# All queues of a fused attention and expert kernel in another written order, with 16 filling products at the start

## The chip, the cores and the metric

The kernel runs on one core of a Trainium2 chip. The metric is device time in microseconds (us) of one execution. Every operation is issued by one of the core's engines: TensorE (PE in the profile, its weight loads PEld), VectorE (DVE), ScalarE (ACT), GpSimd (POOL) and SyncE (SP, which only issues DMAs here; ScalarE and GpSimd issue some too).

## What is computed

```python
# q, k, v: 8 batches, 8 heads, 576 positions, 64 dimensions
scores = q @ k.T / 8                       # per head
local   = (rel >= 0) & (rel < 32)          # heads 0..3, rel = query - key
strided = (rel >= 0) & (key % 32 == query % 32)   # heads 4..7
x = softmax(where(mask, scores, -1e9)) @ v        # x: 8 x 576 x 512, heads side by side
logits = x @ w_gate                        # 4 experts, the best 2 of each token
for e in range(4):                         # a causal attention head of 64 dimensions each
    y = softmax(causal(x @ wq[e] @ (x @ wk[e]).T / 8)) @ (x @ wv[e]) @ wo[e]
    out += weight[e] * y                   # softmax over the two best logits, 0 for others
```

## The kernel before

The work of a batch falls into two stages. Stage 1 handles heads in pairs (`hp` 0 to 3; 0 and 1 local, 2 and 3 strided). Queries and keys are loaded, turned so that the head dimension lies on partitions (`load_big`, `tp`, `tp_out` for batch 0 and part of batch 1; VectorE's `turn` or `turn_s`, L574, for the others), and multiplied block by block (`s_l`, `s_s`). In batches 0 and 1 the mask is added by a product in the same bank ahead of the scores (`pre`, L646). The row softmax has six steps: `softmax0` maximum (VectorE), `softmax1` subtraction, `softmax2` exponential (ScalarE, L697), `softmax3` sum, `softmax4` reciprocal (both VectorE), `softmax5` scaling (L708, on VectorE or GpSimd in batches 0 and 1, on GpSimd later). The probabilities are turned by VectorE (`turn`, L722) or TensorE (`pt`, `pt_out`), multiplied by the values (`xa_l`, `xa_s`) and split into a rounded part `xh` and a rest `xl`.

Stage 2 multiplies these by the expert weights, which are split in the same way (`hi_w`, `lo_w`, L453 and L456): `pj` for queries and keys (three products for each K tile), `vp` for values and gate. `gate1` (GpSimd), `gmax`, `gate2`, `gate3` (VectorE, L907 to L909) and `gate5` (GpSimd) make the experts' weights. `s2` are the scores, `max2`, `exp2`, `recip2` and `scale2` their softmax, `t2` the transposes, `acc` the product with the values, `oh` and `ol` its split, `yp` the product with `wo` and `store` the output.

Nothing is scheduled by a planner at run time. Each operation gets a number when it is declared (`op`), and the text `PLAN` lists all of them in one order. A word such as `85P1511` is operation 85 on TensorE (P; A is ScalarE, D VectorE, G GpSimd, S SyncE) and the buffer numbers that it takes, one digit for each new buffer. `schedule` walks the list, so each engine's queue has its operations in the order of the words with its letter, and waits come from the dependencies. Engines work in order: a waiting operation holds all behind it. Copies out of PSUM may stand on ScalarE or VectorE, loads on SyncE, GpSimd or (the first) ScalarE.

`warm` (2) is a row of products on constants that stands first on TensorE; it reads `fz`, which `one` (0) sets on VectorE. It writes the eight banks, then six of them again, 328 columns each. `fill` operations (2625 and up; `NF` of them) are single products of 448 columns whose result nobody reads. They stand in the list wherever its writer put them.

```python
    def spin(i):
        wb = RB.new(f"spin{i}")
        op("fill", "P", 448, 0, lambda e: ones(wb, 448), r=[fz], w=[wb], mode=M128)
```

Of the kernel before, what the change touches and what calls it, by code (L numbers as in the profile page):

```python
# [20 lines left out]
def attention_moe_kernel(  # L21
# [72 lines left out]
    NF = 26  # L94
# [26 lines left out]
    def issuer(e):  # L121
# [13 lines left out]
        2643P1 2644P1 2645P1 2646P1 2647P1 2648P1 2649P1 85P1511 160A 183S2 121D 159A 52D 122G 148S 228P240 54D  # L135
        86A 88A 230D 179G0 123P760 89D 180S 225P34 87D 192G 125A 1209P50 226A 124D 227A 1202P1 162D 195S3 150G
        229D 126P6322 191D0 149S 184A 1246P71 127A 131D 292G1 129A 161D 1260P4 186S 181A 236P2 208G1 163D 237P0
        182D 363S2 193A 130D 128D 90G 132D 165G 151S 1210P 239D0 164G 241D 1247P 293S 238D 1203P 185G 194D
        1266P6 146S 290G 166P321 187A 212S 1261P 167A 168D 328G3 196A 198S 1211P 240D 287G 1248P 188D 288S 197D
        1267P 205S 286G 169P3233 291S 209G 213A0 1204P 330S 172A 174A 173D 170A 1253P0 331G 329S 175D 242A 1254P  # L140
        171D 202G 1255P 243D 1222P2 365S 1256P 327G4 244D 325S 1262P 199A 1212P 300S2 200G 1216P3 1214A0 1205P
        214G0 1257A 294D1 231S1 206A 1268P 324G 1223P 210A 1206A 1269P 295D 369S0 1258A1 207G 1249P 1207A 326S
        1224P 1270A 337G0 1271A 302P0 1213D 255S1 303P1 1250D 304P0 203A 1251D 253S 211D 340P5 472G1 1217P 306D1
        204D 1225P 368S 20G012345 305D 1263P 232S 1272D0 1252G 1233P70 307D 1264A 473S 1227A 333D0 1226A 367G
        1259G 1235P6 308D 434S3 332D 176G 309A 245G 366S 1218P 1236A 341P0 1265D 1234A 397S4 342P1 435G 310D
        299S 1273P1601 55G 344D2 133G 233G 1361P740 334S 1228D1 19D0 346D 254G 297S 343D 1229P2 1363D0 1215G
# [1102 lines left out]
```

## Time and profile before

| | us |
|---|---|
| median of 3 runs | 432.48 (432.35 to 433.54) |
| the profiled execution | 432.82 |
| its span, first to last instruction | 431.1 |
| TensorE busy | 421.2 |
| VectorE busy | 344.3 |
| GpSimd busy | 322.6 |
| ScalarE busy | 241.5 |

Times in the rows count from the start of the span. Matmuls are pipelined, and their ends are modelled: a row's duration is longer than the time that the next product waits for it, and a started matmul can make TensorE look busy while the following one waits. Durations of VectorE and ScalarE operations overlap their neighbours' by some 0.08 us. A row of the timeline with "x14" is a run of 14 instructions, and its second figure is the time from the first one's start to the last one's end. In square brackets stands the idle time before a row and what ended it. "PEclk" is the granted TensorE clock as a share of full speed.

### The profile page before, as it was taken

How to read it: one execution, taken by the hardware profiler on the slowest of the kernel's cores; microseconds unless marked ns; L12 is line 12 of the kernel's file. 1: busy time of each engine (PE TensorE's matmuls, PEld its weight loads, DVE VectorE, ACT ScalarE, POOL GpSimd, SP SyncE). 2: the span in 40 equal slices, each digit the busy share in tenths (PEclk: the TensorE clock that was granted, in tenths of full speed). 3: DMA queues.
4: the chain of work that ended last, by engine and by line, in shares of the span. 5: the costliest groups of instructions: out<-in, count | busy, mean ns of one | idle time of the engine just before them, and what ended most of it. 6: DMA issues, size and time to landing. Idle time of an engine off the chain costs nothing.

```text
span 431.1 us, 18683 instructions
## 1 busy us (share of the span) xinstructions
PE 421.2 (98%) x7506; PEld 369.0 (86%) x7506; DVE 344.3 (80%) x1046; ACT 241.5 (56%) x753; POOL 322.6 (75%) x554
## 2 busy tenths in 40 slices
PE   8899998999999999999999999999999999999996
PEld 5679877999788988899888997999898998997875
DVE  2897999899998799999898989766998768453734
ACT  3555277654964567545774355626791367466840
POOL 7899876999996978898799925996888232935900
PEclk9999999999999999999999999999999999999999
DMA  8986755564745625774433615245221100003014
GB/s 178 214 171 127 144 120 98 114 128 91 132 88 96 142 55 127 158 145 80 85 79 65 148 33 123 63 117 120 65 58 61 50 26 2 2 26 100 27 75 147
DMA packets 145951, 41.78 MB, mean 97 GB/s; under 512 B 137600, under 2 KB 139008, under 8 KB 145864
## 3 DMA queue, kind: packets, MB, share of 16 engines
q1 hardware_dynamic: 139416, 32.05, 35.6%
q0 software_dynamic: 5856, 8.39, 7.9%
q8 instruction: 59, 0.97, 1.0%
q14 instruction: 28, 0.23, 0.2%
q10 hardware_dynamic: 592, 0.15, 0.1%
HBM read 31.11 MB, written 9.44 MB: 94 GB/s over the span
## 4 chain that ended last, share of the span: by engine, by line
PE 87%; DVE 5%; POOL 3%; issue 1%; DMA 1%; ACT 1%; SPq 1%; POOLq 0%; DVEq 0%; ACTq 0%
PE bank L936 21%; PE bank L1171 12%; PE bank L857 10%; PE bank L1136 10%; PE bank L1038 8%; PE bank L1103 7%; PE bank L780 3%; PE bank L803 2%; PE bank L635 2%; PE bank L628 2%; PE bank L990 2%; PE bank L865 2%; PE bank L732 2%; PE bank L947 1%; PE bank L760 1%
## 5 line engine op out<-in xcount | busy, mean ns | idle before, releaser
L1084 POOL TENSOR_SCALAR p<-p,st,wt 128x128 f32<-128x128 f32 (+3 forms) x128 | 76.5, 606 | 6.6 <-DVE st L1064 5.4
L1056 ACT ACTIVATE p<-p,st 128x128 f32<-128x128 f32 (+3 forms) x128 | 72.1, 567 | 14.0 <-DVE st L1051 14.0
L1051 DVE CUSTOM_DVE_ANT_0 p<-bank,m_cau 128x384 f32<-128x384 f32 (+3 forms) x128 | 57.1, 480 | 4.5 <-PE bank L1038 2.8
L574 DVE STREAM_TRANSPOSE qkt<-nat 128x576 f32<-128x576 f32 x52 | 52.9, 1026 | 1.4 <-issue 1.4
L324 ACT COPY th<-bank 128x256 f32<-128x256 f32 (+2 forms) x121 | 46.2, 444 | 11.9 <-PE bank L1103 8.7
L1136 PE MATMUL bank<-th,vs 128*64 128x192 f32 (+4 forms) x512 | 48.0, 337 | 0.1
L1136 PEld LDWEIGHTS bank<-th,vs 128*64 128x64 f32 x512 | 34.2, 137 | 14.3 <-issue 8.0
L857 PE MATMUL bank<-wh_v,xh 128*128 128x260 f32 x128 | 36.7, 286 | 0.0
L857 PE MATMUL bank<-wh_v,xl 128*128 128x260 f32 x128 | 36.3, 283 | 0.0
L857 PE MATMUL bank<-wl_v,xh 128*128 128x260 f32 x128 | 36.2, 283 | 0.0
L746 DVE TENSOR_TENSOR xl<-bank,xh 128x270 fp32r<-128x270 f32 (+4 forms) x104 | 32.4, 337 | 3.2 <-ACT xh L324 2.8
L1103 PE MATMUL bank<-ident,p 64*128 64x64 f32 x800 | 34.0, 228 | 0.7 <-POOL p L1084 0.6
L936 PE MATMUL bank<-xh,wh_k 128*128 128x288 f32 x112 | 34.2, 305 | 0.0
L1103 PEld LDWEIGHTS bank<-ident,p 64*128 64x128 f32 x800 | 29.4, 138 | 5.3 <-ACT th L324 0.9
L936 PE MATMUL bank<-xh,wh_q 128*128 128x288 f32 x112 | 33.5, 299 | 0.0
L936 PE MATMUL bank<-xl,wh_k 128*128 128x288 f32 x112 | 33.0, 295 | 0.0
L936 PE MATMUL bank<-xl,wh_q 128*128 128x288 f32 x112 | 33.0, 295 | 0.0
L936 PE MATMUL bank<-xh,wl_k 128*128 128x288 f32 x112 | 33.0, 295 | 0.0
L936 PE MATMUL bank<-xh,wl_q 128*128 128x288 f32 x112 | 33.0, 295 | 0.0
L324 ACT CAST qk<-bank 128x288 fp32r<-128x288 f32 x37 | 14.8, 404 | 29.7 <-PE bank L936 27.0
L965 POOL TENSOR_TENSOR qkl<-kf,qk 128x288 fp32r<-128x288 f32 x32 | 25.7, 809 | 2.2 <-DVE kf L324 1.9
L1171 PE MATMUL bank<-wh_o,oh 128*128 128x512 f32 (+1 forms) x66 | 26.5, 401 | 0.0
(191 smaller groups left out, 1330.8 us busy)
## 6 DMA issues: line engine op xcount, KB each, us to landing
out_dram<-ys SPq DMA_DIRECT2D x31, 256.0 KB
nat<-in_k_dram SPq DMA_DIRECT2D x74, 72.0 KB
nat<-in_q_dram SPq DMA_DIRECT2D x72, 72.0 KB
v<-in_v_dram SPq DMA_DIRECT2D x60, 40.0 KB
nat<-in_q_dram POOLq DMA_DIRECT2D x32, 72.0 KB, 3.0
v<-in_v_dram SPq DMA_DIRECT2D x96, 22.5 KB
nat<-in_k_dram POOLq DMA_DIRECT2D x30, 72.0 KB, 3.2
v<-in_v_dram SPq DMA_DIRECT2D x56, 27.0 KB
```

Source lines behind the costliest of these rows:

```text
L324: (nc.scalar.copy if e == "ACT" else nc.vector.tensor_copy)(dst, src)
L574: nc.vector.transpose(dst, src)
L746: op("xl", "D", n_, key + 0.5, lambda e, s_=s_, x_=x_: nc.vector.tensor_sub(x_(xl.t), s_(xa.t), x_(f(xh.t))), r=[xa, xh[u]], w=[xl[u]])
L857: nc.tensor.matmul(vp.t[:m, :NV], xx.t[:, t0:t0 + m], ww.t[:, kt, :], start=i == 0, stop=i == 11)
L936: nc.tensor.matmul(pj.t[:, :HS], ww.t[:, kt, ep * 128:(ep + 1) * 128], xx.t[:, c], start=i == 0, stop=i == 11)
L1038: nc.tensor.matmul(sp[a].t[:, c0:c0 + nk], x.t[r, 0, q0:q0 + 128], y.t[r, 1, :nk], start=i == 0, stop=i == 2)
L1051: lambda e, sp=sp, p=p, a=a, nk=nk, ci=ci, c0=c0: nc.vector.tensor_tensor_reduce(out=p.t[:, a, :nk], in0=sp[a].t[:, c0:c0 + nk], in1=m_cau ...
L1056: op("exp2", "A", nk, k_ + 1, lambda e, p=p, a=a, ci=ci, nk=nk: nc.scalar.activation(p.t[:, a, :nk], p.t[:, a, :nk], AF.Exp, bias=st.t[:, ...
L1084: lambda e, p=p, a=a, ci=ci, t=t, nk=nk: nc.gpsimd.tensor_scalar(p.t[:, a, :nk], p.t[:, a, :nk], st.t[:, 14 + ci + a:15 + ci + a], wt.t[:, ...
L1103: nc.tensor.transpose(tp[hf].t[:, 64 * c:64 * c + 64], src, f(ident.t[r, r]))
L1136: nc.tensor.matmul(acc.t[o, c0:c0 + cn], vw, th[a].t[:, s0:s0 + cn], start=j == 0, stop=j == idx[-1], skip_group_check=True)
L1171: nc.tensor.matmul(yp.t[:, :w_], xx.t[:, c0:c0 + 128], ww.t[:, ep, c:c + w_], start=i == 0, stop=i == 5)
```

## The change

Three places change. `NF` becomes 36, so there are ten more fillers. `warm` writes all eight banks twice: 16 products instead of 14. And `PLAN` is replaced as a whole: the same operations in another order on every engine, some on another engine. VectorE has 819 operations instead of 811, ScalarE 608 and seven loads instead of 609 and one, GpSimd 409 instead of 411, SyncE 331 instead of 336. Counted by kind, VectorE takes more of `softmax5` (5 instead of 2), `pt_out` (12, 6), `vp_out` (20, 15), `pj_out` (31, 27) and `kf` (8, 6), and fewer of `xh` (38, 44), `t2_out` (36, 39) and `tp_out` (6, 8). Of the ten added fillers none stands ahead of `xa_l` 85; six stand right behind it and five (where one stood) ahead of `s2` 1275 and `xa_s` 316.

```diff
-    NF = 26
+    NF = 36
     PLAN = """
-        23A0 12G0 24S 4D0 0D0 5G 22S 2P01234567 21S 14G01 7A 15G012 6A 57S1 8A 59S 9G 3G0 56S 58G 92S0 36P0 70P1
-        35P2 139G0 95S1 93S 17G0123 2625P3 2626P3 28P340 91G 25P56 94S 30A 26A 27D 96S 137G1 29A 10D00 2627P7
-        37P0 32S0 134G 16D01 135S 71P7 38D0 136G 138S 60P451 63P63 40D 61A 34G 65D 42A 39D 64A 18G0 62D 44D
-        2628P2 2629P2 72P1 13D0 41D 31G 33S 43A 108S1 73D1 67G2 74D 2630P2 2631P2 2632P2 100P240 45D 69G 177S0
-        97P36 101A 46D 76D 68S 48G 110P5 99A 235P0 98D 109P2 47G 221S0 102A 75D 78A 66G 49D0 2633P7 2634P7
-        2635P7 111P0 77A 224G 152P7 113D2 79D 189S1 11G 143P631 140P14 145A 144D 103S 105G 142A 80D 50P6300 112D
-        141A 81D 222S 115D 82G 153P4 51D 223S 117A 154P1 114D 107G 178A0 83D 116A 155D3 156D 119D 201G0 104S
-        158D 118D 289G0 84D1 106S 147G0 190A0 120D 53A 157D 2636P1 2637P1 2638P1 2639P1 2640P1 2641P1 2642P1
...
-        1305P261 262A 348D 1364A 1331P5700 258D 259A 1306D 301S 247P0144 1242D00 1308A 471G 349D 1336D2 298S
-        1219P 1307D 248A 264G1 1243A 313P421 250A 266S 1244D 1220A 350G 267P6 296S 314A 370D 1312A 268P4 269P1
...
+        22A0 138S0 4D0 10D00 5G 95A1 0D0 2P01234567 17G0123 21G 6A 24A 16G01 23G 8A 59A1 94A0 11G 134A1 14G01
+        3G0 7A 56A 15G012 28P010 9G 107S0 25P23 30A 29D 96G 35P4 27A 71P5 57S 36P6 26A 70P7 58G 37P0 93S 18G0
+        92S 38D0 91S 40D 137G 2625P1 110P1 109P0 39D 42A 41D 139G 44D 136S 201G0 135S 2626P3 2627P3 2628P3
+        63P321 208G1 60P46 65A 64D 68S1 43A 61D 62A 20G012345 45D 33S2 2629P2 2630P2 97P230 13D0 46D 66G 72P1
+        34S 99A 98D 31G 32S 100P46 74D1 186G0 67S 101A 76D 69S 102D 2631P3 2632P3 140P321 104G 143P54 73D 153P6
+        145A 141D 111P0 142A 47D 224G0 177S1 78A 152P4 112D2 144A 75D 221S 48G 80D 2633P3 2634P3 2635P3 154P1
+        77A 180G 49D0 222S 235P3 114D 189G2 50P2500 223S 79D 116A 113D 287S0 81D 115D 82G 108S 118D 117A 83G
+        156D3 51A 155D 103S 105G 119D 84D1 120D 192G 157D 2636P7 2637P7 2638P7 2639P7 2640P7 2641P7 2642P7
+        2643P7 2644P7 2645P7 2646P7 2647P7 2648P7 2649P7 85P7011 183S 181A0 53D 178A 121D 106S 179G0 52D 54D
+        292G1 122D 150S2 2650P1 2651P1 2652P1 2653P1 2654P1 2655P1 225P140 148G 86A 88A 1209P20 198S3 87D 227A
+        182D 1246P51 226A 158D 123P740 147G 89D 160A 228P16 159A 202S 1202P0 162D 124A 1203P 125D 151G 193A0
+        326S2 1247P 161D 229A 190A 236P7 329S3 163D 126P4122 230A 164D 187A 205S 286G 184A 165D 237P0 131A 291S
...
+        543S0 370D 336S 247P6144 1368A 1337D 270D 271D3 334S 1333D 350G 313P351 272D 250A 1243A 273D 263S0 1365A
+        251D 2656P0 2657P0 1275P0411 401G4 314A 1244D 315A 266S 1340P130 274D 1245G 1313D 472S 275A 376P520
...
     def warm(e, bs):
-        for x in [*bs, *bs[:6]]:
+        for x in [*bs, *bs]:
             ones(x, 328)
```

## Rows read from the trace of the kernel before

**Rows 1.** The page: totals of each engine, and shares of the chain of waits

```profile
PE 421.2 (98%) x7506; PEld 369.0 (86%) x7506; DVE 344.3 (80%) x1046; ACT 241.5 (56%) x753; POOL 322.6 (75%) x554
...
PE 87%; DVE 5%; POOL 3%; issue 1%; DMA 1%; ACT 1%; SPq 1%; POOLq 0%; DVEq 0%; ACTq 0%
```

**Rows 2.** Stages: length, busy (count) of PE, PEld, DVE, ACT, POOL; clock, DMA, GB/s

```profile
24.60:57.30 32.70, 32.48 (x567) 29.47 (x569) 28.68 (x72) 14.85 (x45) 29.64 (x52) 1.00 0.78 149
57.30:74.70 17.40, 15.38 (x450) 12.91 (x446) 16.72 (x56) 13.33 (x43) 12.26 (x22) 1.00 0.49 99
74.70:215.00 140.30, 140.30 (x2791) 125.51 (x2788) 127.54 (x378) 85.92 (x272) 124.34 (x195) 1.00 0.56 111
215.00:230.00 15.00, 14.23 (x353) 11.97 (x353) 13.47 (x44) 10.52 (x32) 14.61 (x24) 1.00 0.35 80
```

**Rows 3.** The same view, between ends of VectorE's operations 84 and 279

```profile
9.52:24.57 15.05, 13.51 (x343) 9.06 (x332) 13.33 (x37) 7.90 (x18) 13.08 (x26) 1.00 0.94 202
24.57:74.23 49.66, 47.39 (x1008) 41.98 (x1010) 44.96 (x126) 27.71 (x85) 41.94 (x73) 1.00 0.68 131
```

**Rows 4.** Chain of waits, 55 to 80 us: start, us, what

```profile
60.41 1.60 DVE sel L907
...
68.37 0.82 PE bank L1103 x17
...
74.81 1.32 PE bank L760 x71
```

**Rows 5.** Timelines of VectorE and of GpSimd: start, us, engine, line, operation

```profile
21.41 0.41 DVE L708 TENSOR_TENSOR p1l<-p1l,st 128x256 f32<-128x256 f32 x1
24.82 0.75 POOL L708 TENSOR_TENSOR p1s<-p1s,st 128x324 f32<-128x324 f32 x1
24.94 0.99 DVE L708 TENSOR_TENSOR p1s<-p1s,st 128x324 f32<-128x324 f32 x1
60.41 1.59 DVE L907 TENSOR_TENSOR sel<-sel,wt 128x20 f32<-128x20 f32 x1 [0.19 <-ACT wt L921]
60.66 1.29 POOL L708 TENSOR_TENSOR p1s<-p1s,st 128x648 f32<-128x648 f32 x1
268.35 0.17 DVE L907 TENSOR_TENSOR sel<-sel,wt 128x20 f32<-128x20 f32 x1
```

**Rows 6.** VectorE's groups by shape: count, busy us, mean ns, idle before

```profile
L691 DVE TENSOR_TENSOR p1s<-bank,st 128x324 f32<-128x324 f32 x8 | 3.8, 471 | 0.0
```

**Rows 7.** Timelines of ScalarE, GpSimd and VectorE up to 9.4 us

```profile
0.80 0.72 ACTq L522 DMA_DIRECT2D vs<-in_k_dram  x1
1.55 1.28 ACT L373 ACT_TABLE_LOAD   x1 [1.55 <-PEq L1233]
5.51 0.99 POOL L522 DMA_DIRECT2D vs<-in_k_dram  x1
8.49 0.54 DVE L362 MEMSET m_cau<- 128x576 f32 x1
```

**Rows 8.** DMA issues: engine, count, KB each, median us to landing

```profile
vs<-in_k_dram POOLq DMA_DIRECT2D x2, 144.0 KB, 4.0
...
p<-in_k_dram POOLq DMA_DIRECT2D x2, 128.0 KB, 5.0
```

**Rows 9.** Timeline of TensorE in the first 28 us

```profile
1.33 4.01 PE L339 MATMUL bank<-fz 128*128 128x328 bf16 x14 [1.33 <-DVE fz L334]
7.09 0.77 PE L542 MATMUL bank<-ident,vs 64*128 64x64 f32 x18
8.65 1.21 PE L616 MATMUL bank<-qkt 64*32 64x64 f32 x72 [0.49 <-ACT qkt L324]
12.32 1.21 PE L616 MATMUL bank<-qkt 64*32 64x64 f32 x72 [0.95 <-DVE qkt L324]
21.67 2.86 PE L339 MATMUL bank<-fz 128*128 128x448 bf16 x14
```

**Rows 10.** Chain of waits, its last TensorE piece

```profile
419.14 8.64 PE bank L1171 x42
```

More of the change, by code (lines that the diff above doesn't have):

```diff
@@ L137, in attention_moe_kernel @@
[L137 to L146, printed above, removed]
@@ new lines, in attention_moe_kernel @@
+        129A 127A 191G0 132D 203A0 146S 130D 128D 166P611 194G 185D 293S 1253P4 168A 149G 1210P 167D 1211P 290S
+        204D0 1204P 188D 195S 330G 239D0 1248P 238D 1254P 209S 1255P 240D 212S 1222P1 241D 289S 169P6333 242A
+        288S 1260P7 172D 174D 325S 196A 199A 173D 1261P 175D 197G 206A 1223P 295D1 170A 1266P3 200G 1267P 327S
+        324G 1262P 171D 243D 1268P 335S1 338G 1256P 244D 1212P 337S 207D 1263P 1214A0 294D 1224P 245G 234S0
+        1213A 210A 302P6 1225P 328S 1258A1 1257D 1249P 254S1 363G4 332D0 1205P 466S1 303P2 1259G0 1207A 304P0
@@ new lines, in attention_moe_kernel @@
+        1449D 417D 608S 1458D 1358P3 418G 607S 1535D 1460A 609S 1480D 1302P6 574G 1359A 611S 453D 1454D 1452A
+        442S 1479D 220G 1451A 1360D 1422P1 1303A 570S0 1536D 1456A 478G 419D1 1414P7 1423A 1455A 1459D 454G
+        519D0 1424P4 420P530133 1425A 1537A 1304D 520G 615D1 1387P20 421A 620S2 423A 425A 1461A 1415D 682S4 426D
+        1426G000 1427D01 572S 491P460 427D 428D 1447P70 576S 424D 493A 422D 1481A 492D 455P131 621S 1504P5611
+        1482A 456D 1462D 494P4100 1428A 1484D 457A 1540D 1538A 458P7311 1505D1 513G0 584S1 1429D 495A 1485A
@@ new lines, in attention_moe_kernel @@
+        1509D 1396P02 544D 497A 521A 1430G 619S 459D 1486D 463A 1393P51 1467G 498D 461A 617S 1397A 462D 464D
+        1487G 1388A 499D 577S 500D 1489G 550P031 677S2 496D 460D 573S 1490P211 1464G 551D 676S 1496P472 1463G
+        552D 1575P01 1497A 1466G 614D 1492A 1488G 1541A 571S 522D 1468G 515S 1583P3 1576A 1577D0 501G 1491A
+        579D0 1498A 1389S 1578G0 1507A 680S 1394A 1465G 622P410 1506D 646S3 1510D 643G1 1469P020 645S 1512A 623D
+        1472P753 644G 578D 649S 1471A 1513P641 1511A 582G 1586P2 1515D 514S 1542D 1514D 678G 1473D 642S 1516A
@@ new lines, in attention_moe_kernel @@
+        1611P0 751S 629D 534D 630G 589D3 618S 532D 1594P7 1593D 585S 1543G 1501D 530D 1503D 712S 1582G 1392S
+        1598P3 1595A 752G 1612A 713S 1608A 1590P4 1588A 547S 714G 1599D 715G 711S 1549P650 750S 1519G 1591A
+        1546P713 1523G 1550A 1552P23 1548D 1551A 1528P461 1554A 1553D 1610G 1525P512 1613A 685D 1633P320 1529A
+        1614G 1527A 1654P041 782S4 1526A 1634D 749G 1530A 1710P150 1632A 1656D3 590G 1627A 631P360 1712D5 616S
+        1596P4 1635D 784G 591A 546S 1655D 1547A 583G 1711D 548S 1600P5 690P200 1601A 1597A 592D 632A 580S 633A
@@ new lines, in attention_moe_kernel @@
+        639A 1665G 818S 637D 1648P041 635A 1559D 659D1 597A 1680P7511 721S2 596A 856G 638D 1650A 636D 1689P611
+        686S 1649A 1685D0 789G 1672P3420 1681D 1690D 762P070 1565S 1673A 785G 697D 1674A 1682D 816S 726P631 640D
+        1687A 698G 764D 788S 598P4211 1691D 823S 1686D 1664G 1645P713 1718D 763D 1566P50 1647A 660G 601D 603D
+        1646A 654S1 599D 1693A 602D 699D0 641G 661A 821S 1651P011 1663G 727D 1684A 653S 600D 1719G 765D2
+        700P176422 604D 790D1 1748P21 705A 761S0 728D 1688A 851G4 707D 662D 1571S 652G 791D 850S 1759P3 1750A0
@@ new lines, in attention_moe_kernel @@
+        828S 1885D 1814G 931D0 1817G 866P721 1734A 1737A 778D 742D 1026S3 1813G 1834A 1818P510 906G 868D 925S
+        1821P633 839D0 1820A 1862P421 827S 1732A 1887A 1029G 1928P11 1863D 923S 1822A 1823D 745G 1028S 860G
+        1819A 1864D 1562S 1733D 867D 840P463544 1835D 805D1 1838G 1924P2 847A 900S2 1735D 1860A 1929D 675G 848D
+        845A 1836G 841D 1886A 901S 843D 930D 849G 1930A0 1824P722 1926A 844D 1033S1 964D1 1865A 1032S 869D3
+        806P051655 1825A 842D 870G 1891D 1932P4 811A 809D 966S1 807A 812D 1866A 1931G0 846D 907A 1867D 1068G4
@@ new lines, in attention_moe_kernel @@
+        1981A 1745P22 2040D 1003G 1950A 1977A 976D 1062S 941A 876D 1739P40 2042A 1951G000 916D 942D 1007D
+        1742P01 1740A 1952D00 1746A 977D 1741S 919A 1972P53 1743D 978G 878P6411 2009D 2065D 1042P201 918D 883A
+        935S0 1005G 920D 881A 2007A 943D 2029P5311 1044D 1980A 2059P170 1067G 2034D 879A 2041A 979D0 1744S
+        1880P000 1953A 1004S 2030D 2031D 2035D 1063S 884D 1904P5 2060D 882D 880D 1043D 885G 980P341622 1905A
+        1954D 2036A 2037A 1955G 2097P21 983A 981D 1036S1 2033A 944G 982D 2010A 1987D 1039S 987D 1906D 2061D
@@ new lines, in attention_moe_kernel @@
+        1179G 1920S 2129P6 2117A 1130S 2159A 2124G000 1134S 2142A 2141A 1181S 2158A 1909P52 2131D 2179A 2125D01
+        1170S 952D 2130D 1171S 2071P140 2143D 1910A 2077P301 2073D 2136G 2072A 1051P670 1911S 2026D 2078A
+        2050P542 2160D 2079A 2132G 1104D 2144P1210 2051A 2052A 2145P30 955G 2237D5 989G 1052A 2181D 2074P54
+        2126A 1053A 2053P263 2238D 2075A 1015P171 2182D 2054A 2076D 2211P051 2055A 2127D 1016A 2232P320 2212D0
+        1017A 2128G 2183A 2202P4611 2234D 2164G 1018P1700 2213D 2166G 2233D 1054P0211 2165G 1021A 1107S2 1019A
@@ new lines, in attention_moe_kernel @@
+        2184D 2203D 1110P531 2185G 2207D 1057A 2214A 1141S1 1023D 2163G 1059D 2215A 2056P400 1024D 1143S 2162G
+        2209A 1112D 2161G 1058D 2239A 1106S 2204D 2187G 1060D 2080P711 1020D 2057A 1140S 2208D 2206A 1108G 1111D
+        1055A 1142S 2058D 2205A 1076P320 1056D 2236A 1145S 1022D 2194P6523 1078D 2170P400 1077D 2196A 1144S
+        2167P121 2195A 1113D0 2188P35 2081A 2273P61 2189A 1138D1 1114G 2235A 2210A 2082D 1079D1 1109G 1115A
+        2309P30 2172D 2190A 2274A 1116D 2168A 1080G 2083A 2085P50 1174D0 2310A 2311A0 2171A 2186G 2169A 2240D
@@ new lines, in attention_moe_kernel @@
+        2313P0 1117D 1081A 2312G0 2086D 2275A1 1082D 1061G 2087S 1025G 1118G 2316P1 1175D 2242G 2216D 2084D
+        2305P3 1083D 2222G 2317D 1119D1 2218G 1084G 1139D 1120P425644 2306A 2314D 2173P722 1125A 1073G2 1074S
+        2315D 1121A 2307A 2319D 2318A 1127D 1075S 1128D 1182P031 1122D 2174A 2217G 1126D 2220G 1146P160 2221G
+        2094P41 1147D 2243G 1184D 1148D 2219G 2175D 2091P52 2308G 2095D 1183D 2096S 2241G 2281P1 1072S 2092D
+        1149D3 2093S 2247P360 1150G 2282A 2191P74 1123A 2378P0500 2283D1 2249A 2192A 2248D 2193A 1085D0 2408P611
@@ new lines, in attention_moe_kernel @@
+        2508A 2507A 2267P30 2262D 2263S 2467P6 2268D 2497D 2561D 2264P21 2468D 2464D 2552D 2473G000 2258P32
+        2265D 2500D 2474D01 2349P511 2259A 2563A 2260S 2269S 2405P000 2350A 2266S 2475A 2499A 2476D 2502A 2351D
+        2420P671 2477G 2406A 2370P1220 2509D 2422A 2426P433 2407D 2421A 2514G 2367P57 2427A 2372D 2493P6010
+        2428A 2511G 2368A 2494P42 2510G 2586D4 2369A 2512G 2371A 2530D3 2364P35 2554A 2423P70 2513G 2525P160
+        2366A 2425D 2555A 2515G 2531D 2365A 2581P501 2565D 2532A 2526D 2568G 2373P422 2527D 2424A 2567G 2528A
@@ new lines, in attention_moe_kernel @@
+        2566G 2587D 2571G 2582D 2529A 2429P333 2569G 2583D 2374A 2376A 2588A 2570G 2533D 2375D 2534G 2572P170
+        2432A 2430A 2584A 2433D 2516P622 2377D 2536G 2431D 2519P501 2573D 2585A 2575P433 2574D 2434P12 2535G
+        2518A 2589D 2517D 2521A 2591G 2520A 2577D 2576A 2443P70 2592G 2435A 2436S 2590G 2437P21 2444A 2445S
+        2440P02 2438D 2439S 2578P622 2441A 2442S 2522P500 2579A 2580D 2596P340 2523A 2593P173 2597D 2598A
+        2599P20 2595A 2524D 2543P6412 2594A 2537P37 2600D 2601A 2540P51 2544D 2542A 2602P0 2541D 2545A 2538D
```

224 lines of the change are left out of this document (85 added, 139 removed).

## The prediction

> **What bounds the kernel now.** I read the page's totals first: TensorE is busy 98% of the span and holds 87% of the chain of waits [rows 1]. Its work is the same in both kernels, apart from fillers, so time can only come from the 2% in which it is not busy and from stretches in which it is "busy" only because a started matmul lies in its pipeline while the next one waits. The busy time by stage shows where these are [rows 2]. Before 24.6 us TensorE waits for the first batch's chain (load, transpose, scores, softmax, values) and runs fillers. From 24.6 to 57.3 it is full. From 57.3 to 74.7 it is busy 15.38 of 17.40 us while VectorE is busy 16.72. From 74.7 on it is full again, but for 0.8 us between 215 and 230, up to the last stores.
>
> So the first 75 us are VectorE's: 13.33 of the 15.05 us from its first row maximum to the transpose that frees `xa_l` 85, then 44.96 of the 49.66 us to the transpose that frees `xa_l` 280 (hp 1 of batch 1) [rows 3]. The chain of waits says the same: from 60.41 to 68.3 it is made of VectorE pieces alone, and it returns to TensorE for good at 68.37 [rows 4]. The largest piece is 1.60 us, `gate3`'s product on 128x20 values. The timeline shows it ending at 62.00, just after GpSimd's 1.29 us `softmax5` ended at 61.95 [rows 5]; the same line takes 0.17 us at 268.35, where GpSimd is quiet [rows 5]. A `softmax5` half on VectorE took 0.99 us beside GpSimd's `softmax5`, 0.41 us beside a GpSimd load [rows 5]. VectorE loses some 2.0 us to this before 75 us: 1.42 on `gate3`, 0.58 on `softmax5`.
>
> **A checkpoint.** I compared the two orders product by product. At `xa_l` 280, which starts at about 74.8 [rows 4], both have issued exactly the same useful products; the new order has ten fillers more. So what the change is worth by then is the change of that one start; it reaches the end unless later stretches add or lose. The sum is made against the profiled execution's 432.82 us (431.1 of span, 1.7 around it).
>
> **Part 1: the start, to `xa_l` 85.** ScalarE now issues seven of the first loads, not one, at 0.72 us each [rows 7]. Its table load (1.28 us, already paid before, from 1.55 [rows 7]) falls behind two of them, and the last of three mask copies (`bandc` 7) behind six: 0.80 + 0.72 + 0.72 + 1.28, then 24, 8, 59, 94 and 134 to about 6.5, copy done at 6.95. GpSimd's `first` waits for it, and behind `first` stand loads 96 and 58. GpSimd also issues 21 and 23 itself; loads of 144 KB from it landed after 4.0 us [rows 8], so 23, issued at about 3.75 (its selections end at 2.33 as before, then load 21 with up to 0.99 [rows 7] and six small memsets), lands near 7.6. The transposes `tp` 28 and 25 go then, not at 7.09, and `s_l` 37 follows the four mask products at about 9.15 instead of 8.65 [rows 9]. Load 58, issued at about 8.1, lands between 11.6 and 13.8 (3.5 to 5.7 us, the nearest rows being 4.0 and 5.0 [rows 8]): `s_l` 72 at 13.1 to 15.2, before 12.32. SyncE's second word, load 107, waits for GpSimd's memset 15, so 57, 93, 92 and 91 start only at about 7 us; this costs no more than 58 does.
>
> VectorE's first maximum so comes at 10.0, not 9.52. From there to the transpose 84 its list is 12.9 us long by the spacing of its kinds of operations, where the old list had 12.8 and waits stretched that to 15.05. With 1.0 us (58's copies, all else ready) to 2.3 us (as before) of waits, 84 ends between 23.9 and 25.2; I take 24.4 against 24.57: **-0.2**. The later start of the first products (VectorE's mask memsets, 0.54 us and a shorter one [rows 7], now stand ahead of the one that they read) and the two added ones (0.27 us each: 14 take 4.01 [rows 9]) end at 6.7, under the wait for load 23: nothing. If that cover goes they cost 0.5.
>
> **Part 2: fillers.** Fourteen take 2.86 us, 0.19 each [rows 9]. Six stand right behind `xa_l` 85, where `pj` 1209 needs `xl` 52 and 54, which VectorE ends some 2 us after the transpose 84 (26.7 before); five, where one stood, are ahead of `s2` 1275 and `xa_s` 316 in the 57-to-75 stretch. Both places wait for VectorE now, and that hides them: 0. Without that cover the ten cost 1.9 us, which is the upper bound; nothing makes a gain of them.
>
> **Part 3: VectorE between 84 and 280's transpose.** The new order gives it 106 operations instead of 101. `softmax5` halves: four instead of one, 3 x 0.41 = 1.2 us where nothing blocks. The rest (`xh` +2, and one more each of a maximum, a subtraction, `max2`, `t2_out`, `pj_out`; three `tp_out`, one `kf` and one `lo_w` fewer) adds 0.9 by the mean durations of its kinds, which are 0.2 to 0.8 and mostly near 0.47 [rows 6]. That is +2.1 us of bare work. The 49.66 us of before were 43.0 of bare work, 2.0 of blocking and 4.7 of idle time (49.66 - 44.96 [rows 3]). `softmax5` 350 now runs right behind `gate1` on GpSimd, and what stands beside `gate3` is a load, so the 1.42 should go. Beside the VectorE halves 122, 164 and 165 stand loads as well; only `lo_w` 179 and 191 are near, and I keep 0.6 for one meeting, like the 0.58 seen. Of the idle time I let 1.7 be filled by the added work and keep 3.0, as it lies in many short waits. So 45.1 + 0.6 + 3.0 = 48.7: **-1.0**. Bounds: all 4.7 of waiting and three halves blocked, 45.1 + 1.7 + 4.7 = 51.5, +1.8; and nothing of either, 45.1, -4.6, of which TensorE can take less: the ten products from `pj` 1219 at 59.65 to `t2` 1323 at 67.98 are worth about 4.8 us by the shortest start-to-start time of each kind in this trace and took 8.3, and 0.8 of the 3.5 lost goes to the five fillers there, so -2.7.
>
> A rule bears on this. The Trainium skill, page "SBUF — State Buffer", section "SBUF: two separate sides", says that VectorE and GpSimd share one port pair under an exclusive lock, that a VectorE operation with two SBUF inputs takes it against a GpSimd operation that reads SBUF, and that the loser waits for the whole instruction. The rows agree in kind (1.59 for 0.17). By that rule each added half could stand behind a whole GpSimd operation; that is the second rival below, priced there from rows.
>
> **Part 4: behind 75 us.** VectorE stays about 3 us of work deeper in its list than before (copies moved from ScalarE, which is 56% busy), but it was idle 12.8 of the 140.3 us to 215 [rows 2], so this is absorbed, and the order of products is largely the old one. The end is the same: the last seven output tiles, 42 products, run without a gap from 419.14 [rows 10], and in the new order too the tiles of ready rows stand between the last `acc` and those that need it. I take 0, bounded by +1.5 (a gap like the 0.8 at 215 to 230 twice over) and -0.8 (that gap gone).
>
> **Sum:** 432.82 - 0.2 - 1.0 = 431.6 as a profiled execution. That execution stands 0.34 over the median of the runs, so the forecast is **431.3**.
>
> **Rivals**, each set against the median, 432.48.
> - *VectorE's waits go too.* For it: many waits before 75 us are for TensorE and ScalarE, which the new order may feed earlier. Against it: VectorE is busy 91% there already. TensorE then decides: -0.2 - 2.7, 429.6.
> - *The added VectorE work shows*, the one on the other side. The halves meet GpSimd's arithmetic and no wait closes: `xa_l` 280 comes 1.8 us later, less 0.2 from part 1, 434.1. Blocking and idle time together must pass 4.8 us of that stretch; they were 6.7 and I forecast 3.6. For it: VectorE is 96% busy from 57.3 to 74.7. Against it: its neighbours in the written order are loads.
> - *The start is late.* Load 58 lands at 13.8, `s_l` 72 goes at 15.2, 2.9 later than before, and all behind it moves along, transpose 84 too: +2.9 - 1.0, 434.4. It decides from 84 ending past 25.6. Against it: most of VectorE's list up to 84 belongs to other pairs.
> - *Nothing that can be measured:* gains and added work cancel at 280, 432.5.
>
> A page's price bears on the late start. The Trainium skill, "DMA: Bandwidth & Descriptors", section "Anatomy of one DMA", fits a GpSimd-issued load as about 2.0 us plus bytes over 436e3 per us; that makes 2.3 for 144 KB, where the row has 4.0, and by it that rival would vanish. The row decides.
>
> **How the numbers follow.** 0.3% (1.3 us) is about what a measurement of this kernel can tell from no change. Forecast 0.38 (430.0 to 432.6: 0.23 faster, 0.15 same), waits go 0.18 (faster), VectorE's work shows 0.16 (slower), late start 0.11 (0.09 slower, 0.02 same), nothing 0.17 (0.13 same, 0.02 on each side). Faster 0.43, same 0.30, slower 0.27. The range runs from the first rival less part 4's 0.8 and 1.0 of an earlier start (23.9 and better), 427.8, to the late start plus part 4's 1.5, 435.9. The forecast's own is 430.0 to 432.6.
>
> **What would show it.** Right: `gate3`'s product at 0.2 us; `xa_l` 85 starting at 24 to 25 us and `xa_l` 280 at 72.5 to 74.5; TensorE busy over 16.4 us in the 17.4 before it. Wrong: `s_l` 72 past 15 us, VectorE `softmax5` halves of 0.9 us or more, or 280 later than 74.8; or 280 where I say and a new gap of over 1 us behind 75 us.

## The result and the profile after

The changed kernel takes 435.58 us (435.01 to 437.17, 9 runs) where the kernel before took 433.36 (432.35 to 434.28, 9 runs beside it): a ratio of 1.0058, interval 1.0041 to 1.0075. It is 2.2 us slower by the medians; the forecast was 431.3. The two profiled executions differ as much (435.03 against 432.82, spans 433.3 and 431.1), so the traces can be set against each other place by place. At these four places both orders have issued the same useful products:

| start of | before, us | after, us | difference | gained or lost since the line above | forecast |
|---|---|---|---|---|---|
| `xa_l` 85 | 24.62 | 26.87 | +2.26 | +2.26 | -0.2 |
| `xa_l` 280 | 74.74 | 76.81 | +2.07 | -0.19 | -1.0 |
| the last 42 products | 419.07 | 420.40 | +1.33 | -0.74 | 0 |
| (end of the span) | 431.11 | 433.32 | +2.21 | +0.88 | 0 |

Two places lose, the start and the end; the middle gains less than I had said by 280, and more behind it.

**The start.** The chain of waits of the changed kernel (start, length, what) runs through a load for 5 us:

```profile
3.72 4.97 DMA vs<-in_k_dram
...
8.73 0.47 PE bank L542 x7
9.22 1.07 ACT qkt L324 x3
10.34 2.04 PE bank L616 x72
...
13.40 0.91 PE bank L339 x3
14.31 0.44 PE bank L542 x8
...
16.19 1.14 PE bank L616 x72
```

The load is 23, the keys of the first pair. GpSimd issues it at 3.72, and the transposes `tp` 28 and 25 wait for it to 8.73. Before, 23 was the first DMA of all and they went at 7.09 [rows 9]. The first scores (`s_l` 37) start at 10.34 instead of 8.65, those of the second pair (`s_l` 72) at 16.12 instead of 12.32; the last line is their piece of the chain, which counts from 16.19. The same view of the DMA issues as in [rows 8], up to 10 us (engine, count, KB each, median us to landing), gives loads 23 and 58 together:

```profile
vs<-in_k_dram POOLq DMA_DIRECT2D x2, 144.0 KB, 5.4
vs<-in_q_dram POOLq DMA_DIRECT2D x1, 144.0 KB, 3.8
```

So 58, issued at 7.69, needed 5.8 us and landed at 13.5. By stage (length, busy and count of PE, PEld, DVE, ACT, POOL; granted clock, DMA share, GB/s) the clock is seen to fall as well:

```profile
6.80:8.70 1.90, 0.29 (x1) 0.10 (x1) 0.00 (x0) 0.00 (x0) 1.76 (x5) 1.00 1.12 191
8.70:10.30 1.60, 1.49 (x21) 1.19 (x21) 0.42 (x1) 1.06 (x3) 1.39 (x5) 1.00 1.33 233
10.30:11.30 1.00, 0.96 (x42) 0.96 (x46) 0.00 (x0) 0.00 (x0) 1.00 (x3) 0.61 1.40 210
11.30:12.40 1.10, 1.10 (x43) 0.93 (x34) 0.79 (x2) 0.00 (x0) 1.10 (x2) 0.50 1.10 153
12.40:13.40 1.00, 1.00 (x4) 0.73 (x5) 0.97 (x4) 0.47 (x1) 0.96 (x8) 0.50 1.35 208
13.40:15.00 1.60, 1.60 (x22) 0.85 (x20) 0.65 (x2) 0.23 (x1) 1.60 (x4) 0.83 1.27 245
```

TensorE did one transpose in the 1.9 us before the load landed; then, between 10.3 and 15.0, its granted clock was down to 0.50, the 1.2 GHz level, for about 3.4 us, and `s_l` 37 took 2.04 us instead of 1.21. The DMA share is 1.1 to 1.4 all the while, much as before (1.17 to 1.24 from 5.3 to 12.3 us), so a loaded DMA system alone does not tell the kernels apart; what differs here is when each load was issued and what was issued ahead of it.

From 8.73 to 85 the chain has pieces of TensorE and ScalarE and none of VectorE. The 25 fillers that both orders have ahead of 85 lie on it for 5.8 us. No run left these out; VectorE was idle for 1.69 us from its first maximum to the end of 84, and 85 came 0.36 us behind that end, so by my estimate they cost at most some 2 us there.

**VectorE up to 280's transpose.** The answers to [rows 3], again from its first maximum to the end of 84 and from there to the end of 279, then the stretch from 57.3 to 74.7 as in [rows 2]:

```profile
11.58:26.51 14.93, 14.69 (x351) 10.09 (x342) 13.24 (x35) 7.16 (x16) 9.88 (x21) 0.92 1.04 190
26.51:76.69 50.18, 49.93 (x1027) 43.49 (x1024) 45.97 (x132) 29.07 (x86) 42.28 (x71) 1.00 0.70 124
```
```profile
57.30:74.70 17.40, 17.37 (x463) 14.54 (x459) 16.96 (x64) 13.71 (x39) 14.51 (x27) 1.00 0.58 103
```

The second stretch is 50.18 us, not 48.7. TensorE looks full from 57.3 on (17.37 of 17.40), but fillers and started products that wait are in that figure; its useful products came no earlier. So this sign of being right (over 16.4 us) came true and said nothing. `gate3` is mended, and a `softmax5` half (165) has its trouble instead (timelines of VectorE and GpSimd, as in [rows 5]):

```profile
32.82 2.40 DVE L708 TENSOR_TENSOR p1s<-p1s,st 128x324 f32<-128x324 f32 x2
...
66.64 0.17 DVE L907 TENSOR_TENSOR sel<-sel,wt 128x20 f32<-128x20 f32 x1
```
```profile
33.44 1.42 POOL L456 TENSOR_TENSOR wl_q<-th,wh_q 128x256 fp32r<-128x256 f32 x2
```

Halves 164 and 165 took 2.40 us together, 165 alone 1.98 (33.24 to 35.22): it stood through two `lo_w` of GpSimd in a row, which end at 34.86.

**The end.** The last 42 products take as long as before (8.66 us, [rows 10]), but SyncE issues the last store 2 us later. SyncE's issues after, then before:

```profile
427.05 0.47 SPq L1180 DMA_DIRECT2D out_dram<-ys  x1
427.57 0.59 SPq L1181 DMA_DIRECT2D out_dram<-ys  x1
428.45 0.47 SPq L1180 DMA_DIRECT2D out_dram<-ys  x1
428.97 0.60 SPq L1181 DMA_DIRECT2D out_dram<-ys  x1
429.66 1.03 SPq L1183 DMA_DIRECT2D out_dram<-ys  x2
```
```profile
421.55 0.47 SPq L1180 DMA_DIRECT2D out_dram<-ys  x1
...
425.71 0.47 SPq L1180 DMA_DIRECT2D out_dram<-ys  x1
426.24 0.59 SPq L1181 DMA_DIRECT2D out_dram<-ys  x1
427.12 1.47 SPq L1183 DMA_DIRECT2D out_dram<-ys  x3
```

Two stores of the last seven have two DMAs each (L1180 and L1181). Before, one of them went early, at 421.55; now both stand right ahead of the last two stores.

### The profile page after: what moved, and what is told of

Read it like the earlier page. It is cut to its first block, busy times and chain, and to the rows that moved or that the text cites. A ratio compares the mean times of both kernels' runs of the same rounds, so it can differ in the third digit from the quotient of the medians.

```text
span 433.3 us, 18748 instructions
## 1 busy us (share of the span) xinstructions
PE 424.3 (98%) x7518; PEld 371.6 (86%) x7518; DVE 349.0 (81%) x1053; ACT 240.9 (56%) x746; POOL 322.3 (74%) x556
## 4 chain that ended last, share of the span: by engine, by line
PE 95%; DMA 1%; DVE 1%; issue 1%; ACT 1%; POOL 0%; POOLq 0%
PE bank L936 21%; PE bank L1171 12%; PE bank L857 11%; PE bank L1136 11%; PE bank L1038 8%; PE bank L1103 7%; PE bank L780 3%; PE bank L635 3%; PE bank L803 3%; PE bank L947 3%; PE bank L628 2%; PE bank L990 2%; PE bank L865 2%; PE bank L339 2%; PE bank L732 2%; PE bank L760 1%
## 5 line engine op out<-in xcount | busy, mean ns | idle before, releaser
L1051 DVE CUSTOM_DVE_ANT_0 p<-bank,m_cau 128x384 f32<-128x384 f32 (+3 forms) x128 | 58.0, 480 | 3.2 <-PE bank L1038 1.4
L324 ACT COPY th<-bank 128x384 f32<-128x384 f32 (+2 forms) x124 | 47.1, 440 | 15.3 <-PE bank L1103 14.7
L597 POOL DMA_DIRECT2D v<-in_v_dram x48 | 30.7, 642 | 1.0 <-PE bank L803 0.4
L324 ACT CAST xh<-bank 128x270 fp32r<-128x270 f32 (+4 forms) x66 | 20.1, 337 | 20.1 <-PE bank L780 10.3
```

Of the source, the lines that this page charges most:

```text
L324: (nc.scalar.copy if e == "ACT" else nc.vector.tensor_copy)(dst, src)
L1051: lambda e, sp=sp, p=p, a=a, nk=nk, ci=ci, c0=c0: nc.vector.tensor_tensor_reduce(out=p.t[:, a, :nk], in0=sp[a].t[:, c0:c0 + nk], in1=m_cau ...
```

## The experiments

Each is a change of `PLAN`'s words; the other words and their order stay. The table has what the traces show; ratios are to the kernel before, run beside each. "VectorE" is the time from the end of 84 to the end of 279, "tail" the time from the first of the last 42 products to the end of the span.

| kernel | ratio (interval) | `s_l` 72 | `xa_l` 85 | VectorE | `xa_l` 280 | tail |
|---|---|---|---|---|---|---|
| before | 1 | 12.32 | 24.62 | 49.67 | 74.74 | 12.04 |
| after | 1.0058 (1.0041 to 1.0075) | 16.12 | 26.87 | 50.18 | 76.81 | 12.92 |
| start of before | 1.0098 (1.0070 to 1.0126) | 12.05 | 24.65 | | 79.12 | 13.11 |
| rest of before | 1.0108 (1.0074 to 1.0142) | 15.79 | 26.34 | | 79.53 | 11.98 |
| tail of before | 1.0041 (1.0022 to 1.0059) | 17.45 | 27.87 | 49.93 | 77.58 | 12.13 |
| no added fillers | 1.0070 (1.0048 to 1.0093) | 16.32 | 27.98 | 49.65 | 76.66 | 12.91 |
| 23 early | 1.0040 (1.0015 to 1.0064) | 15.11 | 25.35 | 49.82 | 75.15 | 12.92 |
| 23 and 58 early | 1.0006 (0.9992 to 1.0021) | 14.07 | 24.32 | 49.83 | 74.09 | 12.93 |
| 58 early | 1.0034 (1.0018 to 1.0051) | 16.20 | 26.45 | 50.02 | 76.43 | 12.92 |
| 58 early, ten fillers | 1.0124 (1.0079 to 1.0169) | 18.71 | 31.13 | 50.18 | 81.27 | 12.93 |
| `lo_w` later | 1.0045 (1.0024 to 1.0067) | 17.39 | 27.80 | 49.36 | 76.99 | 12.91 |
| all mended | 0.9992 (0.9969 to 1.0015) | 13.86 | 24.10 | 49.42 | 73.47 | 12.14 |
| before, `gate3` alone | 0.9970 (0.9951 to 0.9988) | 12.18 | 24.31 | 49.32 | 74.07 | 12.05 |
| before, `gate3` and 58 | 0.9957 (0.9944 to 0.9971) | 13.70 | 25.83 | 48.54 | 74.81 | 11.98 |

**Both starts with both rests.** The lists were cut at `xa_l` 85 and joined the other way round; operations that stand ahead of the cut in one list and behind it in the other follow the list that comes second.

```diff
-(after, to the word ahead of 85P)   (after, from 85P)
+(before, to the word ahead of 85P)  (after, from 85P)     start of before
+(after, to the word ahead of 85P)   (before, from 85P)    rest of before
```

> The order of before (14 warm products, its 25 fillers) up to xa_l 85, the order of after from there. Theory 1, the start alone costs 2.26 us and what follows is worth -0.19 by xa_l 280, -0.74 more by the last 42 products and +0.87 after them: xa_l 85 at 24.6, xa_l 280 at 74.5, last 42 products at 418.2, ratio to before 1.000 (432.42 for a before of 432.48). Theory 2, the rest of the new order pays for its own work on VectorE and only looks cheap because it begins late (loads and copies ran ahead while TensorE was held up): xa_l 280 at 75.5 or later, ratio 1.002 to 1.004.

> The order of after (16 warm products) up to xa_l 85, the order of before from there. Theory 1: the 2.26 us of the start pass through to the end, xa_l 85 at 26.9, last 42 products at 421.4, ratio 1.005. Theory 2: the 2 us in which TensorE waits between 57 and 75 us in before swallow a part, last 42 products at 420, ratio 1.002.

Both theories missed: either mixture is slower than both kernels. The chain of waits of the first shows a place where it loses:

```profile
25.59 0.66 POOL th L443
26.25 5.00 DMA th<-in_moe_wk_dram
```

The new order issues two loads of `wk` (180 and 186) from GpSimd at 18.9 and 14.1 us, ahead of 85, the old one from SyncE behind it; the mixture issues them at 26.3 and 25.5, and `xa_s` 126 goes at 36.30 instead of 33.18. The other mixture was not followed so far. These two runs tell nothing of the start: a cut through all queues leaves out what one side was to do for the other. From here I changed one thing at a time.

**The tail.** The order of the last seven tiles, with their copies and stores.

```diff
-2613P 2610P 2607P 2270P 2622P 2619P 2616P
+2270P 2610P 2607P 2622P 2613P 2619P 2616P
```

> The changed kernel, with the last seven output tiles and what belongs to them in the order of before. Theory 1, two stores of two DMAs each stand late in SyncE's queue and hold the last stores back: the last 42 products start at 420.5 as in after, but the span ends 0.87 us earlier, at 432.4; ratio to before 1.0038. Rival, the end is set by when a store lands and not by its issue: span 433.3, ratio 1.0058.

SyncE's last issues in this kernel:

```profile
429.19 0.47 SPq L1182 DMA_DIRECT2D out_dram<-ys  x1
429.72 0.59 SPq L1183 DMA_DIRECT2D out_dram<-ys  x1
430.61 1.47 SPq L1185 DMA_DIRECT2D out_dram<-ys  x3
```

As theory 1 had it: the tail is 12.13 instead of 12.92 us, in this kernel and in the mended one (12.14), while the eight with the changed tail lie between 12.91 and 13.11. The ratios' intervals overlap; the traces settle it. (The execution shown began 1.0 us later, and its start of the last 42 products was at 422.57, not the 420.5 expected.)

**The fillers.** The eleven behind 85 are left out.

```diff
-2650P1 2651P1 2652P1 2653P1 2654P1 2655P1
...
-2656P0 2657P0
...
-2658P7 2659P7 2660P7
```

> The changed kernel without the 11 fillers behind xa_l 85 (before has one there). My prediction's theory, VectorE's waits hide them: xa_l 280 stays 49.9 us behind xa_l 85, ratio 1.0058 as in after. Rival, TensorE is the bound there by now, and each costs its 0.19 to 0.22 us: xa_l 280 some 2.1 us earlier, ratio 1.001. A part hidden (the six behind xa_l 85, which are followed by a wait for 52 and 54 in any case) and a part not (the five in the 57 to 75 stretch): 1.0 us earlier, ratio 1.0035.

VectorE's stretch is 49.65 us, 0.2 to 0.5 less than in the five runs with the fillers and the same order (49.82 to 50.18). `xa_l` 280 came only 48.68 us behind 85, but because 85 was 1.18 us behind its transpose there (in the products just ahead, TensorE had stood still for 0.69 us for which the profile shows no wait). The time is no better than the changed kernel's. So the fillers cost at most some 0.5 of the 2.1 us that they take: mostly hidden, as I had said.

**The two loads.** First the exchange of 23 and 95, then also that of 58 and 134, then the latter alone.

```diff
-22A0 138S0 4D0 10D00 5G 95A1
+22A0 138S0 4D0 10D00 5G 23A
...
-21G 6A 24A 16G01 23G
+21G 6A 24A 16G01 95G1
...
-94A0 11G 134A1 14G01
+94A0 11G 58A 14G01
...
-70P7 58G 37P0
+70P7 134G1 37P0
```

> The changed kernel with one exchange: load 23 (keys of pair 0) takes the place of load 95 as ScalarE's second DMA, and 95 takes 23's place on GpSimd. Theory A, the first products wait for load 23 because it stands ninth in a DMA system that is full: tp 25 at 7.0 instead of 8.97 and s_l 37 at 8.5 instead of 10.34; but load 58 still lands at 13.5, so s_l 72 only at 15.4 and xa_l 85 at 26.2, ratio to before 1.004. Rival B, the clock that fell to half between 10.7 and 13.9 us is what is late: with no gap of TensorE it stays up, s_l 72 at 14.5, xa_l 85 at 25. Rival C, neither: 85 at 26.9, 1.006.

> The same and load 58 (keys of pair 1) in the place of 134 as ScalarE's last load, 134 in 58's on GpSimd. Theory A: s_l 72 at 12.5 to 13, xa_l 85 at 24.6 to 25, and the 2 us reach the end: ratio 1.001. Rival, VectorE's own list sets 85, not the loads: 85 at 26.5, ratio 1.005. Rival, 134 is now late itself (scores 154): 85 at 25, xa_s 169 later than 39.5, ratio 1.003.

TensorE's timeline with 23 early, then with both:

```profile
6.85 0.86 PE L544 MATMUL bank<-ident,vs 64*128 64x64 f32 x18 [0.48 <-POOL v L317]
...
8.55 1.21 PE L618 MATMUL bank<-qkt 64*32 64x64 f32 x72
...
13.27 0.77 PE L544 MATMUL bank<-ident,vs 64*128 64x64 f32 x17 [1.17 <-DMA vs<-in_k_dram]
...
15.11 1.21 PE L618 MATMUL bank<-qkt 64*32 64x64 f32 x72
```
```profile
8.84 1.21 PE L618 MATMUL bank<-qkt 64*32 64x64 f32 x72
...
12.14 0.84 PE L544 MATMUL bank<-ident,vs 64*128 64x64 f32 x18 [0.90 <-DMA p<-in_k_dram]
...
14.07 1.21 PE L618 MATMUL bank<-qkt 64*32 64x64 f32 x72
```

Theory A holds for the products: with 23 early the first scores go at 8.55 at full clock, and the second pair's transposes then wait for 58 until 13.27; with both early 85 starts at 24.32, ahead of before's, and the whole loss is gone (1.0006), though the tail still has its 0.9 us. Rival B fails at `s_l` 72, which still went at 15.1 with the clock up. At 85 it did not fail: 25.35 is nearer to its 25 than to theory A's 26.2. Moving 23 lifted the wait and the clock together, and no run parts the two. `s_l` 72 at 14.07 is later than the 13 that I expected, and 85 comes earlier all the same; what absorbed the rest was not followed. The wait before 12.14 is put down to a load of `p`, which these transposes do not read; of their own loads 56 was issued last, at 7.11, which may be the next one to move.

> The changed kernel with load 58 in 134's place on ScalarE (134 in 58's on GpSimd), load 23 left where the change put it. If the two loads add up (23 alone brought xa_l 85 from 26.87 to 25.35, both to 24.32): tp 25 still at 9 to 9.7, but s_l 72 at 14.5 to 15, xa_l 85 at 25.5 to 26, ratio 1.003 to 1.004. If 58 alone sets it: 85 at 24.3 to 24.8, ratio 1.001.

Neither came: `s_l` 72 went at 16.20. TensorE takes its words in order; with 23 late it comes to the second pair's transposes only at 14.32, later than 58 had landed in the changed kernel. One late load hid the other, so 58 is worth 0.4 us alone (26.45 against 26.87, less than executions differ) and 1.0 behind 23.

In that kernel TensorE again idled (2.13 us) and fell to the lower clock. Ten fillers were meant to close the gap:

```diff
-28P010
+28P010 2625P6 2626P6 2627P6 2628P6 2629P6 2630P6 2631P6 2632P6 2633P6 2634P6
```

> The kernel of the run only_58_early with ten more fillers (1.9 us) between the transposes tp 28 and tp 25, where TensorE was idle 2.13 us before load 23 landed and where its clock then fell to half for some 3 us. Theory, in that kernel the slow clock is on the path (s_l 37 took 2.15 us instead of 1.21, the three fillers behind it 0.75 each row as before): with the clock up, s_l 72 at 15.2, xa_l 85 at 25.5, ratio 1.001 to 1.002. Rival, the fillers delay tp 25 by what they save, or the clock was not on the path: xa_l 85 at 26.4, ratio 1.0034.

```profile
6.74 0.35 PE L544 MATMUL bank<-ident,vs 64*128 64x64 f32 x1
9.38 0.46 PE L544 MATMUL bank<-ident,vs 64*128 64x64 f32 x7 [2.29 <-DMA vs<-in_k_dram]
9.78 3.07 PE L341 MATMUL bank<-fz 128*128 128x448 bf16 x10
12.78 0.79 PE L544 MATMUL bank<-ident,vs 64*128 64x64 f32 x10
```

This run does not answer its question: `tp` 28 itself waits for load 23 after its first transpose, so the fillers stood behind the wait, not in it, and took 3.07 us of the path, two thirds of it at the lower clock. The ratio was 1.0124 (1.0079 to 1.0169), `xa_l` 85 at 31.13, 4.7 us later than without them; another 1.95 us of that is a pause inside `s_l` 72 (to 21.75) for which the profile shows no wait. What the low clock costs where no load hides it stays open.

**`lo_w` away from the half.** GpSimd's words:

```diff
-286G 191G0 194G 149G 330G
+286G 149G 330G 191G0 194G
```

> The changed kernel with GpSimd's two lo_w (191, 194) moved behind its loads 149 and 330, away from VectorE's softmax5 half 165, which took 1.98 us beside them. Theory: 165 takes 0.5 us, pt 166 starts 1.5 us earlier, VectorE's 84 to 279 shrinks from 50.2 to 49.2 or less and xa_l 280 comes 1.0 to 1.5 us earlier behind xa_l 85: ratio 1.003. Rival, TensorE has enough projections there and VectorE catches up in its idle 4.2 us: 165 short, 280 the same, ratio 1.006.

VectorE's halves 164 and 165, GpSimd's two `lo_w`, two `lo_w` of VectorE beside them, and VectorE's stretch:

```profile
33.75 0.90 DVE L710 TENSOR_TENSOR p1s<-p1s,st 128x324 f32<-128x324 f32 x2
```
```profile
36.38 1.61 POOL L458 TENSOR_TENSOR wl_q<-th,wh_q 128x256 fp32r<-128x256 f32 x2
```
```profile
36.40 1.00 DVE L458 TENSOR_TENSOR wl_k<-th,wh_k 128x256 fp32r<-128x256 f32 x1
...
37.73 0.55 DVE L458 TENSOR_TENSOR wl_v<-p,wh_v 128x260 fp32r<-128x260 f32 x1
```
```profile
27.52:76.88 49.36, 49.23 (x1026) 42.97 (x1024) 45.37 (x132) 28.97 (x86) 42.58 (x71) 1.00 0.71 125
```

The halves take 0.90 instead of 2.40 us, and the stretch is 0.5 to 0.8 us shorter than in the five runs named above, less than the 1.0 that the theory had at least; `xa_l` 280 and the ratio are not told apart from the changed kernel's. The rest did not go into VectorE's waits: it was idle 3.99 us (49.36 less 45.37), 4.21 in the changed kernel. It went into two other blocks. GpSimd's `lo_w` now stand beside two `lo_w` of VectorE, which took 1.00 and 0.55 us; in the changed kernel, beside loads, they took 0.41 each. So 0.73 of the 1.50 us came back a few operations later.

**The kernel before, with `gate3` alone.** GpSimd's words, in the order of before:

```diff
-1241G 471G 264G 350G
+1241G 350G 471G 264G
```

> The kernel before with one move: GpSimd's softmax5 350 right behind gate1, its loads 471 and 264 behind that, so that a load stands beside gate3. Theory of the prediction: gate3's product takes 0.2 to 0.4 us instead of 1.59, s_l 269's follower and the products behind it come 1.2 us earlier, xa_l 280 at 73.4 to 73.8, ratio 0.997. Rival, VectorE's next wait takes it: xa_l 280 at 74.7, ratio 1.000.

```profile
60.97 0.38 DVE L908 TENSOR_TENSOR sel<-sel,wt 128x20 f32<-128x20 f32 x1 [0.19 <-ACT wt L922]
```
```profile
57.30:74.70 17.40, 16.56 (x498) 14.10 (x496) 16.72 (x59) 14.54 (x47) 12.67 (x25) 1.00 0.56 112
```

The product takes 0.38 instead of 1.59 us, the ratio is 0.997 (0.9951 to 0.9988): 432.39 us against 433.43. `xa_l` 280 started at 74.07, 0.67 earlier, not 0.9 to 1.3; 0.31 of it stood at 85 already. So VectorE's stretch gained 0.35 (49.32 for 49.67) of the 1.21 that `gate3` gave back. In this execution the `softmax5` half soon behind 84, which the move does not touch, lost 0.84 of it:

```profile
24.64 1.84 DVE L709 TENSOR_TENSOR p1s<-p1s,st 128x324 f32<-128x324 f32 x1
```
```profile
24.65 0.78 POOL L709 TENSOR_TENSOR p1s<-p1s,st 128x324 f32<-128x324 f32 x1
25.34 0.78 POOL L457 TENSOR_TENSOR wl_k<-th,wh_k 128x256 fp32r<-128x256 f32 x1
```

It took 0.99 us in the kernel before [rows 5]; here it stood through GpSimd's `softmax5` and the `lo_w` behind it. The move also brings 350 forward (60.03 for 60.66 us), so the ratio belongs to the whole move and not to `gate3`'s block alone.

**All together.** The changed kernel with both loads, the `lo_w` and the tail mended; and the kernel before with `gate3`'s move and load 58 as ScalarE's second DMA.

```diff
-23A0 12G0 24S
+23A0 58A 12G0 24S
```

> The changed kernel with all its mends: 23 and 58 early, the two lo_w behind the loads, the last seven tiles in the order of before. If they add: xa_l 85 at 24.3, xa_l 280 at 73.6 (0.5 under the run with the two loads early), last 42 products at 417.6, 12.1 us from there to the end, span 429.8; ratio to before 0.997 (1.0006 less 0.0019 and 0.0012). If the tail's or the lo_w's gain is taken by a wait: 0.9985 to 1.0006.

> The kernel before with two moves: softmax5 350 right behind gate1 (0.997 alone) and load 58 as ScalarE's second DMA, ahead of its table load, instead of GpSimd's at 5.5 us. If the loads of pair 1 bound the start here too: tp 60 at 8.7 to 9 instead of 10.1, s_l 72 at 11 to 11.5, xa_l 85 at 23.8 to 24.2, ratio 0.996. If other loads get pushed back for it (23 shares the DMA engines with it): tp 25 at 7.5 or later, 85 at 24.6 or later, ratio 0.997 to 0.999.

In its trace the mended kernel does what was expected, term by term: 24.10, 73.47, 417.45, a tail of 12.14, span 429.6. That execution, 431.30, is its fastest; the median is 432.77 (431.3 to 436.36), and the ratio, 0.9992, is not clear of 1 and lies where the second expectation had it. What the slower ones wait for was not profiled. The other kernel has the best median, 431.73 (431.45 to 433.14), 0.9957. In the execution shown (432.66) moving 58 cost time at the start, `tp` 25 going at 8.49 and 85 at 25.83: ScalarE's second DMA pushes its table load from 1.55 to 2.24 us, the mask copies with it, and TensorE's mask products from 5.49 to 6.19. That it adds anything to `gate3`'s move is not shown, as the two intervals overlap.

## Why the prediction was wrong

**The step that failed is part 1**, forecast at -0.2, measured at +2.26. It named both issues rightly (23 at about 3.75, found 3.72; 58 at about 8.1, found 7.69), and took the landings too short: 23 "near 7.6" was 8.69, 5.0 us after its issue, and 58 came at the upper end of what was given, 5.8 us after. VectorE's first maximum therefore came at 11.58 instead of 10.0; 0.4 us of that is `s_l` 37 at the lower clock (1.24 us from its start to the maximum, 0.87 before). From there VectorE needed 14.93 us to the end of 84, within the 13.9 to 15.2 that was said but 0.5 over the 14.4 that was taken, and 85 came 0.36 us behind that end, right behind the fillers, where it had been 0.05 before. So the term that failed is the landing of 23: it was given 0.5 us at the first maximum (10.0 for 9.52) and cost 2.1 there, the clock included. Moving 23 alone gave back 1.5 of the 2.26 us, the clock's part included.

One reading under that term was wrong. The prediction has SyncE's 57, 93, 92 and 91 start at about 7 us, behind load 107's wait for a memset. SyncE issued 107 at 1.62, 57 at 2.91, 93 at 3.74 and 92 and 91 from 4.39: four loads of 128 and 144 KB that the prediction did not have beside 23 were on their way with it. How much of the 1.1 us this makes, no run shows.

The rival *the start is late* came true in size (434.4 for +1.9; measured +2.2 by the medians, +2.26 at 85) and half in mechanism: it was made of load 58 alone, and I gave it 0.11. The Trainium skill, page "DMA: Bandwidth & Descriptors", section "Anatomy of one DMA", from whose fit the estimate of 2.3 us for such a load was worked out, is further off here than the row of before (4.0) was: 5.0 and 5.8 us were measured, and the measurement decides.

**Part 2** held: the added fillers cost at most 0.5 us.

**Part 3**, forecast at -1.0 on VectorE's stretch, was +0.5. Its largest reason was right: `gate3`'s block went (1.59 to 0.17), and the move that removes it makes the old kernel faster by itself. Two terms were mis-sized. Blocking was put at 0.6 for one meeting of a half with `lo_w`; the meeting came, with two `lo_w` in a row, and took 1.5 (2.40 less 0.90). Idle time was put at 3.0 and was 4.2. Bare work was less than thought (45.97 less 1.5, so 44.5 instead of 45.1), although the price of an added half was too low: 0.41 was that of a 128x256 one [rows 5], while the added ones are 128x324 and took 0.48 where nothing blocked. By the Trainium skill, page "SBUF — State Buffer", section "SBUF: two separate sides", the loser waits for the whole instruction. The trace agrees, and more: the half waited for two instructions in a row.

**Part 4**, put at 0, was two things: -0.74 in many small steps between 280 and the last products, of which none was tested by itself, and +0.88 in the tail. "The end is the same" looked at TensorE's products and not at SyncE's queue, where the order of the stores had changed.

## What to carry to other kernels

In a crowded start the size of a load does not tell when it lands: in the changed kernel three loads of 144 KB from GpSimd took 3.8, 5.0 and 5.8 us, and two of 32 KB took 6.0 in the median. What the first products read must be issued first; whether a load's place in the line, its time of issue or its issuing engine decides, these runs do not part. A load that is hidden behind another is only seen once that one is mended. When a tail's order changes, follow the stores through their queue and not only the products. And when a blocked operation is moved away from GpSimd's arithmetic, look at what that arithmetic meets in its new place: of 1.50 us won by `lo_w` 0.73 went to two new blocks, and of 1.21 won at `gate3` 0.84 went, in the execution shown, to a half elsewhere.

## What had not been expected of the hardware

Executions of one order differ by a microsecond at fixed places. `tp` 25 behind GpSimd's load 23 went between 8.88 and 9.74 us in six traces, and `xa_l` 85 between 26.34 and 27.98. At 91 us a load of values arrives in time in some executions and not in others; with the tail of before (chain of waits) it did not:

```profile
87.71 0.49 SPq L592
...
88.25 3.66 DMA v<-in_v_dram
```

From `xa_l` 280 to `s_l` 410 this kernel, the one without fillers and the one with 58 early took 18.7 to 19.1 us, the others with the changed middle 17.9. The old order showed 17.8 in every trace. Two pauses of TensorE, 0.69 and 1.95 us, stand inside rows of equal products, with no wait that the profile shows. And the row of the granted clock can miss a stretch: in the kernel with the tail of before, `s_l` 37 took 2.15 us, about what it took at the lower clock, while its row says 1.00.
